# Attention: the products with the values of two steps issued together, every other step

## The chip, the cores and the metric

The kernel runs on one core of a Trainium2 chip. The metric is the device time in microseconds (us) of one execution. TensorE (PE in the profile; its weight loads are PEld), VectorE (DVE), ScalarE (ACT), GpSimd (POOL) and the queue of SyncE (SP) each work through their own list of instructions in order, and wait for one another through semaphores.

## The reference

Three stages follow each other: an attention within clusters, a gated feed-forward layer, and a mixture of eight experts. The change is in the first:

```python
mask = q_assign[:, :, :, None] == k_assign[:, :, None, :]      # clusters by the nearest centroid
scores = scale * np.matmul(q, k.transpose(0, 1, 3, 2))          # batch 2, 8 heads, 768 tokens, 64 wide
scores = np.where(mask, scores, -1000000000.0)
scores = scores - np.max(scores, axis=-1, keepdims=True)
attn = np.exp(scores)
attn = attn / (np.sum(attn, axis=-1, keepdims=True) + 1e-09)
return np.matmul(attn, v).astype(np.float32)
```

All of it is float32.

## The kernel before, in words

The attention works on pairs of heads: 2 batches times 4 pairs, eight in all. A pair's work is cut into 12 steps, two halves of 384 queries (`r`) times six blocks of 128 keys (`t`), so there are 96 steps. `plan` writes the order out by hand: `at(s, f, ...)` appends a piece of work to step `s`, and `advance` issues the steps one after the other, the pieces of a step in the order in which they were appended.

What a step issues, in order:

- `max_unit` (L332), 11 steps ahead of its use: two products `pm` (L344) of 128 queries with 768 keys, and on VectorE the row maximum `m` of them (L348).
- `score` (L369): four products `pst` (L379, L382), two for each head, and on ScalarE the exponential `P` (L386) out of PSUM into an SBUF tile. `P` has four buffers.
- `pv` (L400) of the step before: the products `acc` of the two heads' `P` with V (L410). Each head's output is 64 partitions of the one PSUM bank `acc`, which collects six steps (t = 0 to 5). A float32 product stands in the trace as two matmuls, so a call of `pv` is four `acc` matmuls. After t = 5 ScalarE copies the bank to `x` (L416).
- `add_up` (L389) of the step before: the running sum of the `P` tiles, on GpSimd, for three of the sixteen halves on VectorE.
- In some steps, `norm1` to `norm3`: the products `psum` with a matrix of ones (L423), of the same form as `acc`, and the reciprocal of the sums, which scales `x`.
- Behind these, the preparation of a later pair of heads, spread over 12 steps: transposes `pt` (L228) with the copy `qh` or `kh` on ScalarE and the subtraction `ql` or `kl` on VectorE, similarity products `psim` (L246), and others. `max_put` (L355) puts the negative maxima where the score products add them.

Two pieces of the feed-forward layer run beside it. `Narrow` turns the float64 weights into float32 with int32 operations `n` on ScalarE and VectorE (L663 to L690). From step 84 on, `Moe.first` issues the first products `ph` (L805) of the feed-forward layer between the steps; there are no more `max_unit` calls by then.

`pm` and `pst` tiles come from one function, which hands out two PSUM buffers of two banks each, in turn:

```python
    def big(self, name):
        self.nbig += 1
        return self.ps.tile([128, 2, 512], F32, tag=f"s{self.nbig % 2}", name=name)
```

The functions that the diff touches and what calls them:

Of the kernel before, what the change touches and what calls it, by code (L numbers as in the profile page):

```python
# [169 lines left out]
class Attention:  # L170
# [292 lines left out]
    def plan(self, N):  # L463

        NP = len(self.pairs)
        NS = 12 * NP
        steps = {}

        def at(s, f, *a):
            if s >= 0:  # L470
                steps.setdefault(s, []).append((f, a))

        for n in range(NS):
            at(n - self.AHEAD, self.max_unit, n)
        for s in range(NS):
            at(s, self.score, s)
        for s in range(NS):
            at(s + 1, self.pv, s)
            at(s + 1, self.add_up, s)
            if s % 6 == 5:  # L480
                for j, f in ((3, self.norm1), (4, self.norm2), (6, self.norm3)):
                    at(s + j, f, *divmod(s // 6, 2))
        for i in range(NP):
            end = 12 * i - self.AHEAD
            for r in range(2):
                at(end + 6 * r + 5, self.max_split, i, r)
                at(end + 6 * r + 6, self.max_put, i, r)
            base = end - 15 if i > 2 else self.B2
            if i > 1:
                at(base - 8, self.load, i, "qk")  # L490
                for j in range(4):
                    at(base + j, self.split, i, "qk"[j // 2], j % 2)
                for j in range(4):
                    at(base + 4 + j, self.sims, i, "qk"[j // 2], j % 2)
                at(base + 6, self.pick, i, "q")
                at(base + 8, self.pick, i, "k")
                at(base + 9, self.onehot_t, i)
                at(base + 10, self.first, i, 0)
                at(base + 11, self.first, i, 1)
                for h in range(2):  # L500
                    for kind in ("qa", "ka"):
                        at(base + 8, self.spread, i, (kind, h))
                    for kind in ("km", "qm"):
                        at(base + 12, self.spread, i, (kind, h))
            if i:
                for j, kind in enumerate(("ql", "qu", "kb", "kl")):
                    for h in range(2):
                        at(max(12 * i - 12, 3) + self.BS * j, self.spread, i, (kind, h))
            if i:
                at(12 * i - 12, self.load, i, "v")  # L510
        for c in range(3):
            at(self.N1, N.load, c)
        slots = [12 * p + w for p in range(NP) for w, m in enumerate(self.SLOTS) for _ in range(m)]
        slots = [w for w in slots if w >= self.N0]
        for c in range(N.CUT):
            s0, s1, s2 = slots[3 * c:][:3]
            for s, g in ((s0 - 1, N.bias), (s1 - 1, N.last), (s1, N.up), (s2, N.sign), (s2 + 1, N.store)):
                at(s, g, c)
            if c + 3 < N.CUT:
                at(s2 + self.NL, N.load, c + 3)  # L520
        return steps
# [1163 lines left out]
```

## Time and profile before

| | |
|---|---|
| time, median of 3 runs (lowest to highest) | 811.0 us (809.21 to 812.89) |
| time of the profiled execution | 809.26 us |
| its span, first to last instruction | 807.4 us |
| TensorE, VectorE, ScalarE, GpSimd busy | 95%, 76%, 58%, 27% of the span |
| mean granted clock of TensorE | 0.984 of full speed |

The attention steps take the stretch from 36.5 to about 298 us of the span. A busy share over the whole span is a mean over stages with different limits, so the attention stage is to be read by itself. Matmuls are pipelined: the duration of one in a row is longer than the distance to the next, and the distance of starts is what a row of matmuls costs. Where a row has "x4", four instructions of a line are merged, and the time is from the first start to the last end.

### The profile page before, as it was taken

To read this page: it belongs to the slowest core of one execution; us is meant where nothing else is said; L and a number is where in the kernel's file an instruction comes from. 1 tells how busy PE (TensorE), PEld (TensorE's weight loads), DVE (VectorE), ACT (ScalarE), POOL (GpSimd) and SP (SyncE) were. 2 spreads that over 40 slices of the span, in tenths; PEclk is the share of its full clock that TensorE was granted. 3 is DMA by queue.
4 is the path that set the end of the run, shared out by engine and by line. 5 is a ranking of instruction groups with operands and counts; after the bars stand their busy time and mean duration, and the time that the engine had idled before them with its cause. 6 is when DMAs were issued, how large, how long until landed. Compare 5 with 4: busy or idle time off the path is not lost.

```text
span 807.4 us, 12395 instructions
## 1 busy us (share of the span) xinstructions
PE 764.9 (95%) x4289; PEld 611.2 (76%) x4290; DVE 617.2 (76%) x1195; ACT 468.1 (58%) x899; POOL 218.4 (27%) x177
## 2 busy tenths in 40 slices
PE   7799899998999998989999999999999999999994
PEld 4465465655655566879889989999898999999993
DVE  5868889887898789999998588788667665566661
ACT  4167577675766675555656444455635566566551
POOL 5056577775777210011000002000131011101110
PEclk9999999999999999999999999999999999999997
DMA  7678878888675528778448058322427867887730
GB/s 162 163 193 240 204 201 230 194 228 206 187 201 147 186 98 311 288 268 333 157 167 290 11 195 270 138 105 64 134 92 227 280 209 225 271 264 220 215 122 22
DMA packets 118720, 155.77 MB, mean 193 GB/s; under 512 B 35033, under 2 KB 82233, under 8 KB 114555
## 3 DMA queue, kind: packets, MB, share of 16 engines
q1 hardware_dynamic: 113994, 131.83, 56.0%
q0 software_dynamic: 4656, 23.09, 7.2%
q8 instruction: 35, 0.57, 0.3%
q14 instruction: 35, 0.28, 0.1%
HBM read 93.65 MB, written 42.24 MB: 168 GB/s over the span
## 4 chain that ended last, share of the span: by engine, by line
PE 68%; DVE 18%; issue 5%; ACT 4%; DMA 3%; SPq 1%; POOL 0%; POOLq 0%; DVEq 0%; ACTq 0%
PE ph L805 12%; PE o L866 11%; PE he L1459 9%; PE y L1492 9%; PE acc L410 5%; PE pm L344 4%; PE pst L379 3%; DVE m L348 3%; PE pst L382 3%; PE psim L246 2%; DVE xl L459 2%; DVE cut L763 1%; DVE n L687 1%; DVE n L820 1%; DVE n L680 1%
## 5 line engine op out<-in xcount | busy, mean ns | idle before, releaser
L763 DVE TENSOR_TENSOR cut<-raw,cut 128x512 fp32r<-128x512 f32 x168 | 110.3, 687 | 27.9 <-ACT cut L762 15.4
L386 ACT ACTIVATE P<-pst 128x768 f32<-128x768 f32 x96 | 77.8, 810 | 63.9 <-PE pst L382 59.6
L398 POOL TENSOR_TENSOR sum<-sum,P 128x768 f32<-128x768 f32 x52 | 102.8, 1978 | 5.4 <-ACT P L386 2.6
L762 ACT ACTIVATE cut<-raw 128x512 fp32r<-128x512 f32 x168 | 98.3, 623 | 4.2 <-DMA raw<-in_moe_w_dram 4.2
L1492 PE MATMUL y<-cut,hy 128*128 128x512 f32 x384 | 99.3, 394 | 0.0
L348 DVE TENSOR_REDUCE m<-pm 128x1 f32<-128x768 f32 x96 | 90.7, 949 | 10.5 <-PE pm L344 10.2
L1459 PE MATMUL he<-xeh,cut 128*128 128x256 f32 x512 | 92.4, 280 | 0.2 <-ACT xeh L1413 0.2
L830 ACT ACTIVATE r<-n,two 128x384 f32<-128x384 f32 x64 | 39.5, 617 | 81.2 <-DVE n L820 80.1
L1459 PEld LDWEIGHTS he<-xeh,cut 128*128 128x128 f32 x512 | 82.2, 188 | 5.5 <-ACT xeh L1413 0.4
L410 PE MATMUL acc<-P,vn 128*64 128x384 f32 x384 | 83.7, 515 | 0.1
L1492 PEld LDWEIGHTS y<-cut,hy 128*128 128x128 f32 x384 | 67.6, 188 | 10.9
L805 PE MATMUL ph<-xh,cut 128*128 128x384 f32 x256 | 67.0, 343 | 6.0 <-DVE t L842 3.6
L1459 PE MATMUL he<-xel,cut 128*128 128x256 f32 x256 | 71.5, 279 | 0.2 <-DVE xel L1414 0.2
L344 PE MATMUL pm<-KA,QA 96*128 96x384 f32 x192 | 57.0, 379 | 14.4 <-DVE m L348 12.1
L379 PE MATMUL pst<-QB,KB 128*128 128x384 f32 x192 | 66.6, 347 | 1.1 <-issue 0.8
L805 PE MATMUL ph<-xh,again 128*128 128x384 f32 x256 | 66.7, 341 | 0.0
L1464 ACT ACTIVATE hy<-he 128x256 fp32r<-128x256 f32 x64 | 24.5, 383 | 70.5 <-PE he L1459 70.5
L382 PE MATMUL pst<-QA,KA 97*128 97x384 f32 x192 | 65.3, 340 | 0.0
L1504 POOL DMA_INDIRECT out_dram<-ye,meta x17 | 18.3, 1078 | 171.6 <-ACT ye L1502 154.0
L1465 DVE SCALAR_TENSOR_TENSOR hy<-he,hy 128x256 fp32r<-128x256 f32 x64 | 27.1, 424 | 43.9 <-ACT hy L1464 43.8
L866 PE MATMUL o<-cut,gh 128*128 128x512 f32 x192 | 59.8, 392 | 1.0 <-DVE rs L438 1.0
L866 PE MATMUL o<-again,gh 128*128 128x512 f32 x192 | 60.3, 395 | 0.0
(229 smaller groups left out, 1654.5 us busy)
## 6 DMA issues: line engine op xcount, KB each, us to landing
raw<-in_moe_w_dram SPq DMA_DIRECT2D x72, 256.0 KB
raw<-in_moe_w_dram SPq DMA_DIRECT2D x36, 512.0 KB
kept<-cut POOLq DMA_DIRECT2D x16, 1024.0 KB, 8.2
again<-kept SPq DMA_DIRECT2D x16, 1024.0 KB
n<-in_moe_w_in_dram SPq DMA_DIRECT2D x16, 512.0 KB
n<-in_moe_w_out_dram SPq DMA_DIRECT2D x16, 512.0 KB
wf<-n SPq DMA_DIRECT2D x32, 256.0 KB
raw<-wf SPq DMA_DIRECT2D x16, 512.0 KB
```

The lines of the kernel that those rows point to most:

```text
L344: nc.tensor.matmul(ps[:, g, 0:384], lhsT=QA[0:96, h, q0:q0 + 128], rhs=KA[0:96, h, 384 * g:384 * g + 384], start=True, stop=True,)
L348: nc.vector.reduce_max(out=st["m", r][:, h, t:t + 1], in_=ps[:, :, 0:384], axis=AX.XY)
L379: nc.tensor.matmul(ps[:, h, 0:384], lhsT=KB[:, h, ks], rhs=QB[:, h, qs], start=True, stop=False)
L382: nc.tensor.matmul(ps[:, h, 0:384], lhsT=KA[0:97, h, ks], rhs=QA[0:97, h, qs], start=False, stop=True)
L398: e.tensor_add(out=st["sum", r], in0=st["P", w - 1] if t == 1 else st["sum", r], in1=st["P", w])
L410: nc.tensor.matmul(acc[64 * h:64 * h + 64, 0:384], lhsT=st["v"][:, h, t, :], rhs=pt[:, h, :], start=(t == 0), stop=(t == self.NK - 1),)
L762: nc.scalar.activation(out=t[:, 0, part], in_=raw[:, part], func=AF.Copy)
L763: self.low.tensor_sub(out=t[:, 1, part], in0=raw[:, part], in1=f32(t[:, 0, part]))
L805: nc.tensor.matmul(ps[:, 0:384], lhsT=w[:, k, :], rhs=x[:, k, sl], start=(k == 0 and j == 0), stop=(k == 3 and j == 2),)
L866: nc.tensor.matmul(self.acc[t], lhsT=g[:, c], rhs=w, start=(f == 0 and j == 0), stop=(f == self.NF - 1 and j == 2),)
L1459: nc.tensor.matmul(ps[:, 0:MAIN], lhsT=w[:, k, :], rhs=x[:, k, :], start=(k == 0 and j == 0), stop=(k == 3 and j == 2),)
L1492: nc.tensor.matmul(st["y"][s], lhsT=g[:, c], rhs=w, start=(f == 0 and j == 0), stop=(f == 7 and j == 2))
```

## The change

In `plan`, the products with V of two steps are issued in one step. Before, step s + 1 issues `pv` of step s. Afterwards the steps with an odd s + 1 issue none, and those with an even s + 1 issue `pv` of s - 1 and of s, one behind the other. `add_up` stays in its step and now comes ahead of `pv`.

```diff
         for s in range(NS):
-            at(s + 1, self.pv, s)
             at(s + 1, self.add_up, s)
+            if s % 2:
+                at(s + 1, self.pv, s - 1)
+                at(s + 1, self.pv, s)
             if s % 6 == 5:
                 for j, f in ((3, self.norm1), (4, self.norm2), (6, self.norm3)):
                     at(s + j, f, *divmod(s // 6, 2))
```

## Rows read from the trace of the kernel before

**Rows 1.** The page: busy us of each engine, share of the span, instructions.
```profile
PE 764.9 (95%) x4289; PEld 611.2 (76%) x4290; DVE 617.2 (76%) x1195; ACT 468.1 (58%) x899; POOL 218.4 (27%) x177
```

**Rows 2.** Waits, 60 to 298 us: waiting <- releaser: us in total, times, longest.
```profile
PEld pm L344 <- DVE m L348: 25.3, 32, 2.9
```

**Rows 3.** Timeline of TensorE, step 58: start us, us, engine line op, out<-in.
```profile
203.52 0.34 PE L379 MATMUL pst<-QB,KB 128*128 128x384 f32 x1
...
204.05 0.34 PE L382 MATMUL pst<-QA,KA 97*128 97x384 f32 x1
204.31 0.87 PE L410 MATMUL acc<-P,vn 128*64 128x384 f32 x4
205.11 0.55 PE L228 MATMUL pt<-ident,qn 128*128 128x128 f32 x3
205.41 0.60 PE L344 MATMUL pm<-KA,QA 96*128 96x384 f32 x2
205.84 0.34 PE L379 MATMUL pst<-QB,KB 128*128 128x384 f32 x1
```

**Rows 4.** Timeline of TensorE, step 62, where psum and acc follow each other.
```profile
214.33 0.87 PE L423 MATMUL psum<-sum,ones 128*64 128x384 f32 x4
215.03 0.81 PE L410 MATMUL acc<-P,vn 128*64 128x384 f32 x4
215.77 0.38 PE L246 MATMUL psim<-cc,qh 128*128 128x256 f32 x1
...
216.58 0.51 PE L344 MATMUL pm<-KA,QA 96*128 96x384 f32 x2
```

**Rows 5.** Timeline of all engines, steps 57 to 59; in brackets, idle time and releaser.
```profile
202.73 0.68 DVE L680 SCALAR_TENSOR_TENSOR n<-n,n 128x512 int32<-128x512 int32 x1
...
204.48 0.81 ACT L386 ACTIVATE P<-pst 128x768 f32<-128x768 f32 x1 [1.01 <-PE pst L382]
204.58 8.06 POOL L398 TENSOR_TENSOR sum<-sum,P 128x768 f32<-128x768 f32 x4
...
204.72 2.23 DVE L687 SCALAR_TENSOR_TENSOR n<-n,n 128x512 int32<-128x512 int32 x1
...
205.69 0.49 ACT L234 ACTIVATE qh<-pt 128x384 fp32r<-128x384 f32 x1 [0.40 <-PE pt L228]
...
206.87 0.55 DVE L235 TENSOR_TENSOR ql<-pt,qh 128x384 fp32r<-128x384 f32 x1
...
207.34 0.94 DVE L348 TENSOR_REDUCE m<-pm 128x1 f32<-128x768 f32 x1
...
208.33 0.62 PE L344 MATMUL pm<-KA,QA 96*128 96x384 f32 x2 [0.34 <-DVE m L348]
```

**Rows 6.** Windows, steps 48 to 59, two steps each: stretch, length, busy us of each engine.
```profile
172.30:177.02 4.72, 4.72 (x29) 3.02 (x29) 3.95 (x7) 3.51 (x7) 4.64 (x3) 1.00 0.52 138
177.02:183.17 6.15, 6.15 (x37) 4.09 (x37) 4.30 (x7) 5.12 (x11) 2.66 (x3) 1.00 0.85 235
183.17:189.72 6.55, 5.80 (x33) 3.88 (x33) 6.38 (x8) 3.76 (x8) 6.39 (x4) 1.00 0.98 238
189.72:198.22 8.50, 6.30 (x29) 3.38 (x28) 6.06 (x9) 3.40 (x6) 4.08 (x3) 0.80 0.79 189
198.22:203.52 5.30, 5.30 (x28) 2.89 (x28) 4.23 (x7) 4.56 (x8) 1.01 (x1) 1.00 0.78 228
203.52:208.79 5.27, 4.93 (x27) 2.99 (x27) 5.27 (x6) 3.29 (x6) 5.02 (x4) 1.00 0.30 53
```
The columns of busy time are PE, PEld, DVE, ACT, POOL; then the granted clock, the DMA share and GB/s.

**Rows 7.** Windows, three of the six pairs in steps 72 to 83, same columns.
```profile
240.54:245.54 5.00, 4.43 (x23) 2.49 (x23) 4.84 (x6) 3.11 (x7) 4.84 (x3) 1.00 0.75 215
...
250.30:254.42 4.12, 4.12 (x22) 2.41 (x22) 2.73 (x4) 3.40 (x6) 3.58 (x3) 1.00 1.03 285
254.42:259.93 5.51, 4.44 (x23) 2.49 (x23) 4.85 (x5) 3.09 (x7) 5.35 (x3) 1.00 0.23 67
```

## Prediction, on record before the changed kernel ran

> **What bounds the kernel now.** I read the page first: TensorE is busy for 95% of the span and VectorE for 76% [rows 1], so a saving on TensorE can count, if nothing else ends last. Then the waits of the attention stage, where the change is: the largest wait of TensorE there is for VectorE's row maximum, 25.3 us in 32 cases [rows 2]. So TensorE sets the pace of most steps, and VectorE that of about a third. Third came TensorE's own timeline in one step [rows 3]. I let a step begin with the first pst product. Step 58 begins at 203.52, and the reader is to see five pieces without a gap: 0.53 us to the last pst product, 0.26 until acc starts, 0.80 until the transposes pt start, 0.30 until pm starts, 0.43 until the next step's first pst product; together 2.32 us.
>
> What hides behind that matters more. Every pm and every pst tile comes from the same two PSUM buffers in turn; a step takes one of each, so pm always gets the one and pst the other, and each is single-buffered. The next pst product can't start before the exponential P of this step is through, and the next pm not before this step's maximum m. P started at 204.48 and took 0.81, so it ended 1.77 us into the step [rows 5]; the next pst started at 2.32. Nobody waits for P today because the products with V and the transposes stand in between. That cover is what the change moves.
>
> **The change, part by part.** Removed, added: no instruction. 48 acc groups move from even to odd places, so each odd step loses its group and each even step has two. No DMA is issued by the moved function; the ScalarE copy of a finished acc stays in its step and comes later in it, and the next group's first product comes a step later than now, so it has more room. The adds change places with the products in the program only: they are on GpSimd or VectorE, whose order stays. P tiles of even steps live one step longer; four buffers hold that, since the products two steps on free them.
>
> *What a group costs.* A lone group costs 0.80, and 0.26 from the last pst product where the pst products follow each other at 0.53/3 = 0.18, so 0.08 for the change of shape: 0.88 leave an odd step [rows 3]. The cost of a second group right behind one is in the trace, since psum has the same form as acc: psum starts at 214.33, acc at 215.03, the next work at 215.77; two groups take 1.44, the second adds 0.64 [rows 4]. (By the start distance it would be 0.70; this is the other bound.) Were TensorE alone the limit, a pair of steps would win 0.88 - 0.64 = 0.24 us, and 48 pairs 11.5 us.
> The Trainium skill says in "TensorEngine Tiling (Array Packing)", Key Properties, that going from one tiling mode to another drains the engine. The trace agrees with its direction: the second group is 0.16 us cheaper than the lone one. By that rule alone the change would bring those 11.5 us; that is the first rival below.
>
> *What an odd step can win.* Without its group it needs 0.53 + 0.18 + 0.43 = 1.14 us and whatever else it holds. But pst of the next step waits for P: 1.77 plus the lag from a release to TensorE. The lag is not seen for P; for m it is 0.05 (m ends at 208.28, pm starts at 208.33) [rows 5], which I take, between 0 and 0.10. So an odd step takes at least 1.82 us. Other work in it of 0.68 us or more fills that; less does not.
>
> *Twelve steps of the steady part*, taken as pairs of an even and an odd step [rows 6]; their extra work repeats every twelve steps.
> - First pair (4.72 us, transposes in both). The odd step's maximum is queued on VectorE behind the subtraction of the transposes made in the even step. From the start of pt: 0.58 to the copy qh, 0.49 for it, 0.05 lag, 0.47 from the subtraction's start to that of m, 0.94 for m, 0.05 lag [rows 5], 0.43 from pm to the next pst product [rows 3]: 3.01 us. Now pt starts 0.53 + 0.26 + 0.80 = 1.59 into the step, and the chain ends at 4.60, inside the pair's 4.72. With two groups pt starts at 0.53 + 0.26 + 1.44 = 2.23 and the chain ends at 5.24: a loss of 0.52.
> - Second pair (6.15): both steps hold six psim products, together 0.81 us a step (215.77 to 216.58) [rows 4], over 0.68, so the odd step gets the full gain: -0.24.
> - Third and fourth pair (6.55 and 8.50): TensorE has idle time in them (5.80 and 6.30 busy), VectorE's queue sets the end. Its int32 operations n are the reason: one takes 0.68 alone (202.73) and 2.23 beside GpSimd's adds of P, which run at 2 us each (204.72) [rows 5]. I take 0. Bounds: both gains of 0.24 and one such hold-up of 2.23 - 0.68 = 1.55 avoided half the time, so about -1.2; or psim's 0.64 later start handed on to VectorE and half a hold-up more, about +1.4.
>   The Trainium skill explains the hold-up in "SBUF — State Buffer", Who interferes with whom: a VectorE instruction with two SBUF inputs and a GpSimd one that reads SBUF exclude each other for a whole instruction. The 2.23 beside 0.68 agrees; it means that small shifts come out in lumps here.
> - Fifth pair (5.30): the odd step has one small product besides, about as long as pt's 0.30. It goes from 2.32 to the floor of 1.82, -0.50; the even one +0.64: +0.14.
> - Sixth pair (5.27, transposes in both): the chain of the first pair, again 5.24: -0.03.
> Sum 0.52 - 0.24 + 0 + 0.14 - 0.03 = +0.39; six such twelves (steps 0 to 71): +2.3 us.
>
> *Steps 72 to 83* have no transposes and no psim [rows 7]. A plain step is 0.53 + 0.26 + 0.80 + 0.43 = 2.02 now (the pair 250.30 to 254.42 has 4.12 and no idle time). Odd: 2.02 to 1.82, -0.20; even: +0.64; +0.44 a pair. In two of the six pairs TensorE idles 0.57 and 1.07 us for VectorE, which swallows it: 0. Four pairs: +1.8 us.
>
> *Steps 84 to 95* have no pm, so pst alternates over both buffers, the floor is gone and each pair wins 0.24; the last two groups follow each other already, since no score comes after step 95. Five pairs: -1.2 us.
>
> *Sum:* 2.3 + 1.8 - 1.2 = +2.9 us. What follows the attention waits for it, since TensorE is busy through to the end, so it goes into the time. The profiled execution took 809.26 us, so one like it would take 812.2. It lies 1.7 below the median of the runs, 811.0, from which I state the forecast: 813.9 us.
>
> **The rivals.**
> *All of it is TensorE's.* The floor and the chain don't bind, and 48 x 0.24 = 11.5 us come off: 799.5. For it: TensorE has no gap in three of the six pairs [rows 6]. Against it: in an odd step of 1.14 us TensorE would have to write to the pst buffer some 0.6 us before ScalarE is through with it. 0.07. It is also what the rule on tiling modes in the Trainium skill ("TensorEngine Tiling (Array Packing)", Key Properties) would give.
> *The hold-ups fall better.* GpSimd's adds start later against VectorE's queue in the third and fourth pair, since the steps before end otherwise; six twelves at -1.2: 813.9 - 7.2 = 806.7. Nothing in the trace tells the direction. 0.10.
> *VectorE's queue becomes the bound* (the other side). In the third and fourth pair VectorE is busy 6.38 of 6.55 and 6.06 of 8.50 [rows 6]; if the psim products, 0.64 later in the even step, arrive when VectorE has nothing else, each twelve loses up to 1.4 there, and 1.0 in the mean gives 813.9 + 6.0 = 819.9. It decides from +0.2 us per twelve on, since +2.9 is near the limit of what counts as slower. With long waits comes the clock: in 189.72 to 198.22, after the two longest waits, the granted clock is 0.80 on average [rows 6]; that is the 1.2 GHz level for 40% of 8.50 us, at most 1.7 us of lost work each time. 0.30.
> *The forecast*, 811 to 818: 0.53.
>
> **How the numbers follow.** A measurement here tells 0.5%, 4 us, from no change. The forecast's case has some three quarters of its chance below 815.1 (+0.5%): 0.40 within, 0.13 slower. The third rival is slower, apart from 0.03; the first is faster; the second is faster in half. Faster 0.12, same 0.48, slower 0.40. The likeliest case's own range is 811 to 818. For 8 in 10 I go to 804, which takes in most of the second rival, and to 822, which takes in the third with one more fall of the clock. The second group at 0.70 instead of 0.64 adds up to 2.9 us, the lag of 0 to 0.10 some 1 us either way; both are inside.
>
> **What the new profile would show.** acc in groups of eight at a spacing of 0.64 to 0.70 us; acc gone from odd steps. Odd steps of about 1.82 us with a wait of pst for P that isn't there now, in steps with little else; odd steps that end on m where transposes came before. Even steps of 2.7 to 4.0 us. Wrong would be: odd steps well under 1.8 us before step 84 (then the floor is wrong and the first rival holds), or a total wait of TensorE for m that grows by more than 5 us, or falls (then the queue of VectorE and GpSimd decides).

## The result, and the profile after

The changed kernel takes 825.36 us (820.05 to 825.85, 3 runs), the kernel before 811.0; the ratio is 1.0141 (95% interval 1.0095 to 1.0186). The whole interval lies above 1: the kernel became slower, by some 1.4%, and the time is above the range of 804 to 822. The profiled execution is the one of 825.36 us.

The page's line on TensorE, to be held against [rows 1]:

```profile
PE 767.7 (93%) x4290; PEld 622.4 (76%) x4290; DVE 616.1 (75%) x1195; ACT 462.5 (56%) x899; POOL 218.9 (27%) x177
```

The same work, a longer span: all engines idle more. The first place to look is a plain odd step and the even one behind it, on TensorE and ScalarE (timeline of the changed kernel, steps 57 and 58; start, us, engine, line, and in brackets the idle time and its releaser):

```profile
211.50 0.34 PE L379 MATMUL pst<-QB,KB 128*128 128x384 f32 x1
...
212.46 0.81 ACT L386 ACTIVATE P<-pst 128x768 f32<-128x768 f32 x1 [1.08 <-PE pst L382]
...
213.32 0.19 PEld L379 LDWEIGHTS pst<-QB,KB 128*128 128x128 f32 x1 [0.32 <-ACT P L386]
213.32 0.44 PE L379 MATMUL pst<-QB,KB 128*128 128x384 f32 x1
213.60 0.34 PE L382 MATMUL pst<-QA,KA 97*128 97x384 f32 x1
...
214.23 1.51 PE L410 MATMUL acc<-P,vn 128*64 128x384 f32 x8
215.67 0.55 PE L228 MATMUL pt<-ident,qn 128*128 128x128 f32 x3
```

Step 57 has no acc. P ends at 213.27, pst starts at 213.32: the step takes 1.82 us, and the bracket names P. In step 58 two groups take 215.67 - 214.23 = 1.44. Both numbers are those of the forecast. One thing is new in this place: the weight load of a pst product that waits starts together with the product (both at 213.32), and the second one starts 0.28 behind the first instead of 0.18.

Then the twelve steps of [rows 6], steps 48 to 59, two by two (columns as there):

```profile
182.96:188.25 5.29, 4.75 (x28) 3.21 (x28) 4.50 (x7) 3.87 (x9) 5.07 (x4) 1.00 0.47 134
188.25:194.15 5.90, 5.90 (x37) 4.12 (x36) 4.31 (x7) 4.11 (x9) 2.41 (x2) 1.00 0.87 242
194.15:201.63 7.48, 5.55 (x34) 4.13 (x33) 6.74 (x8) 4.11 (x9) 6.64 (x4) 1.00 0.89 220
201.63:207.77 6.14, 4.60 (x28) 2.77 (x28) 6.06 (x9) 2.71 (x5) 2.27 (x2) 1.00 0.66 164
207.77:213.32 5.55, 5.48 (x27) 2.93 (x26) 4.39 (x6) 4.44 (x9) 2.84 (x2) 1.00 1.02 248
213.32:218.71 5.39, 4.75 (x28) 3.26 (x27) 3.95 (x7) 3.15 (x6) 4.72 (x3) 1.00 0.46 122
```

First, second, fifth and sixth pair came out at 5.29, 5.90, 5.55 and 5.39 where 5.24, 5.91, 5.44 and 5.24 were worked out. The third doesn't fit: 7.48 against 6.55, where I had taken 0. TensorE is busy for 5.55 of it. The fourth can't be compared exactly: the clock fell there in the kernel before [rows 6] and not now. But that fall cost at most the 1.7 us of the prediction, so at full clock the pair took 6.8 us or more before and takes 6.14 now: it became shorter.

Whole twelves, so that the clock can be kept out. First the kernel before (steps 24 to 35, 36 to 47, 60 to 71, 72 to 83, and the ten steps 84 to 93):

```profile
106.55:138.98 32.43, 31.59 (x176) 19.80 (x176) 28.04 (x41) 23.19 (x42) 22.85 (x14) 1.00 0.86 228
138.98:172.30 33.32, 31.84 (x176) 19.74 (x176) 30.13 (x42) 24.10 (x43) 24.68 (x16) 1.00 0.89 221
208.79:240.54 31.75, 31.00 (x169) 19.19 (x169) 27.11 (x39) 22.55 (x41) 22.41 (x14) 1.00 0.77 207
240.54:268.91 28.37, 26.66 (x131) 15.18 (x131) 25.94 (x30) 19.15 (x32) 19.94 (x12) 1.00 0.58 173
268.91:291.41 22.50, 22.47 (x114) 13.20 (x113) 16.33 (x26) 16.31 (x28) 4.58 (x5) 1.00 0.51 188
```

The changed kernel, the first two and the last of these stretches:

```profile
114.22:148.61 34.39, 30.89 (x175) 20.43 (x175) 27.96 (x41) 23.07 (x43) 23.97 (x16) 1.00 0.85 222
148.61:182.96 34.35, 30.79 (x175) 20.41 (x175) 28.37 (x42) 22.94 (x43) 23.89 (x14) 1.00 0.85 206
286.57:308.18 21.61, 21.26 (x114) 14.06 (x114) 16.26 (x26) 15.66 (x27) 4.33 (x5) 1.00 0.52 195
```

All of these rows are at full clock. The twelves lose 1.96 and 1.03 us, where +0.39 was forecast; the last stretch wins 0.89, where 1.2 was. The waits of TensorE for the row maximum, of the changed kernel from 60 to 315 us, answer to [rows 2] and show where the rest of the loss ends. In the first line, the kernel before once more, the wait as the products themselves see it; then the changed kernel:

```profile
PE pm L344 <- DVE m L348: 10.9, 11, 2.2
```

```profile
PEld pm L344 <- DVE m L348: 36.1, 35, 2.5
PE pm L344 <- DVE m L348: 23.5, 26, 1.9
PEld pst L379 <- ACT P L386: 4.7, 18, 0.3
```

The wait for P, which wasn't there, is 4.7 us in 18 cases; the wait for m grew from 25.3 to 36.1 us for the weight loads and from 10.9 to 23.5 us for the products. A growth of more than 5 us was the forecast's own sign that the queue of VectorE and GpSimd decides. So the main loss stands at VectorE's maximum, not at the floor.

**What the clock does to a time here.** The span ahead of step 0, where both programs are the same, was 36.52 us before and 39.10 after, and 39.50 in a later run of the changed kernel (e12). The granted clock goes with it: 0.95, 0.83 and 0.80. It isn't the change that does this: e9, an experiment on the kernel before, whose program is the same up to there, took 39.37 us at 0.75, and e5, with the change, 37.36 us at 0.87. One window each, before and e9; the clock is the third number from the end:

```profile
0.00:36.52 36.52, 27.20 (x138) 17.29 (x139) 24.48 (x61) 11.41 (x27) 11.20 (x19) 0.95 0.73 155
```

```profile
0.00:39.37 39.37, 32.50 (x138) 21.68 (x140) 24.76 (x60) 11.28 (x27) 11.18 (x19) 0.75 0.70 151
```

The mean clock of a run is in every result. The 73 runs of the kernel before that ran beside the experiments go from 807.87 us at 0.988 to 824.4 at 0.957; the straight line through them passes 814.8 us at 0.975 and rises by 5.3 us for each 0.01 that the clock falls, with a scatter of 1.2 us; without the two runs of them that count as slow it moves by less than 0.3 us. Below, "at equal clock" is the mean distance of a kernel's runs from that line. The three runs of the changed kernel lie 8.0 us above it. Their mean clock is 0.973; that of the three runs of before isn't recorded but for the profiled one, 0.984, and their median, 811.0, is where the line stands at 0.982. So of the 14.4 us, some 8 are there at equal clock and some 6 come with the clock.

### The profile page after: what moved, and what is told of

Same layout as the page of the kernel before. It is cut to its first block, busy times and chain, and to the rows that moved or that the text cites. A ratio compares the mean times of both kernels' runs of the same rounds, so it can differ in the third digit from the quotient of the medians.

```text
span 823.6 us, 12396 instructions
## 1 busy us (share of the span) xinstructions
PE 767.7 (93%) x4290; PEld 622.4 (76%) x4290; DVE 616.1 (75%) x1195; ACT 462.5 (56%) x899; POOL 218.9 (27%) x177
## 4 chain that ended last, share of the span: by engine, by line
PE 62%; DVE 19%; issue 8%; ACT 6%; DMA 2%; SPq 1%; POOL 1%; POOLq 0%; ACTq 0%; DVEq 0%
PE ph L807 11%; PE o L868 11%; PE he L1461 8%; PE y L1494 8%; PE acc L410 5%; DVE m L348 4%; PE pm L344 3%; PE pst L379 2%; PE pst L382 2%; PE psim L246 2%; DVE cut L765 2%; DVE n L822 1%; PE psum L423 1%; ACT r L832 1%; DVE xl L459 1%
## 5 line engine op out<-in xcount | busy, mean ns | idle before, releaser
L765 DVE TENSOR_TENSOR cut<-raw,cut 128x512 fp32r<-128x512 f32 x168 | 110.3, 687 | 27.6 <-ACT cut L764 14.4
L386 ACT ACTIVATE P<-pst 128x768 f32<-128x768 f32 x96 | 77.6, 809 | 73.8 <-PE pst L382 67.3
L344 PE MATMUL pm<-KA,QA 96*128 96x384 f32 x192 | 59.4, 393 | 26.7 <-DVE m L348 25.4
L410 PE MATMUL acc<-P,vn 128*64 128x384 f32 x384 | 74.7, 511 | 0.1
L379 PE MATMUL pst<-QB,KB 128*128 128x384 f32 x192 | 70.4, 367 | 1.8 <-issue 1.5
L382 PE MATMUL pst<-QA,KA 97*128 97x384 f32 x192 | 67.3, 350 | 0.0
L344 PEld LDWEIGHTS pm<-KA,QA 96*128 96x128 f32 x192 | 30.8, 200 | 45.8 <-DVE m L348 39.1
```

The source lines that it names most:

```text
L344: nc.tensor.matmul(ps[:, g, 0:384], lhsT=QA[0:96, h, q0:q0 + 128], rhs=KA[0:96, h, 384 * g:384 * g + 384], start=True, stop=True,)
L379: nc.tensor.matmul(ps[:, h, 0:384], lhsT=KB[:, h, ks], rhs=QB[:, h, qs], start=True, stop=False)
L382: nc.tensor.matmul(ps[:, h, 0:384], lhsT=KA[0:97, h, ks], rhs=QA[0:97, h, qs], start=False, stop=True)
L410: nc.tensor.matmul(acc[64 * h:64 * h + 64, 0:384], lhsT=st["v"][:, h, t, :], rhs=pt[:, h, :], start=(t == 0), stop=(t == self.NK - 1),)
L765: self.low.tensor_sub(out=t[:, 1, part], in0=raw[:, part], in1=f32(t[:, 0, part]))
```

## The experiments

| run | kernel | median us | ratio to before, 95% interval | at equal clock, us |
|---|---|---|---|---|
| e1 | changed, idle products in the waits | 831.74 | 1.0242 (1.0183 to 1.0301) | +20.1 |
| e2 | before, without most of GpSimd's adds | 798.8 | 0.9829 (0.9755 to 0.9903) | -14.8 |
| e3 | changed, without the same adds | 803.14 | 0.9869 (0.9807 to 0.993) | -8.6 |
| e4 | groups together in steps 71 to 84 only | 823.23 | 1.0136 (1.0078 to 1.0194) | +5.2 |
| e5 | changed, acc last in its step | 822.97 | 1.0145 (1.0095 to 1.0195) | +7.7 |
| e6 | before, acc last in its step | 815.25 | 1.0025 (0.9986 to 1.0064) | +1.9 |
| e7 | groups together from step 85 on only | 812.4 | 0.9984 (0.9948 to 1.0021) | -1.9 |
| e8 | changed, norm2 first in its step | 826.52 | 1.0179 (1.0136 to 1.0222) | +9.5 |
| e9 | before, norm2 first in its step | 812.68 | 0.9996 (0.9966 to 1.0027) | -2.2 |
| e10 | e7 and e9 together | 812.21 | 0.9962 (0.9927 to 0.9996) | -2.6 |
| e11 | e10, and together around step 3 of each twelve | 816.38 | 1.0015 (0.9984 to 1.0047) | -0.6 |
| e12 | the changed kernel again | 823.96 | 1.0172 (1.0131 to 1.0213) | +7.7 |

Three theories were to be told apart: A, the floor of the odd steps and the chains behind moved products cost more than worked out; B, VectorE's queue is held up longer behind GpSimd's adds; C, the longer waits let the clock fall. Each column of the table has its own weakness: the ratio contains where the clock fell, the last column rests on the line. Steps at full clock, read from the trace, need neither; where they decide, they are shown.

**e1: idle products in the waits of the changed kernel.** Is it the falling clock?

```diff
+    FILL = {1: 2, 5: 6, 6: 6, 9: 2, 11: 2}
...
+        for s in range(NS):
+            n = self.FILL.get(s % 12, 0) if s < 72 else (6 if s == 78 else 3 * (s % 2)) if s < 84 else 0
+            if n:
+                at(s, self.K.warm, n, None)
```

> The changed kernel with idle products (zeros, no use) put into TensorE's waits of the attention: two at the end of odd steps with little work, six at the end of the two steps in which it waits longest for the row maximum, three in odd steps from 73 on. They take 0.22 us each. Theory C (the fall of the clock in those waits costs 5 to 8 us of the 14): no stretch at 1.2 GHz between steps 13 and 84, the time 818 to 821 us. Theory B (the queue of VectorE and GpSimd costs it, the clock little): time 824 to 828, since the waits are as long as before.

Measured: 831.74 us, worse than either theory said. The clock's mean went up to 0.98, and still the kernel stands 20 us above the line. The idle products need a PSUM bank and got one that was still being read, as in step 57:

```profile
218.41 0.60 PE L50 MATMUL warm<-idle 128*128 128x512 bf16 x2 [0.54 <-DVE rs L438]
```

They waited for VectorE to read the bank, and pm, next in the queue, came late (218.66). The run doesn't price the clock, then, since the waits of the idle products can't be told from the change's own loss; it shows that a wait with in-order work behind it is no free room.

**e2 and e3: without GpSimd's adds.** Is it VectorE's hold-ups behind them?

```diff
-        if t == 0:
+        if t == 0 or t > 1 and s // 6 not in self.QUICK:
             return
```

> The kernel before, leaving out GpSimd's running sum of P from the third block of keys on (the sum is that of two blocks only). It takes away what holds VectorE's operations up. Theory B: TensorE's wait for the row maximum falls from some 36 us to under 12, the time to 800 to 804. Theory A (VectorE is simply full): little change, 808 to 812.

> The changed kernel, leaving out the same adds. To be read against e2. Theory B (the change costs by hold-ups of VectorE behind GpSimd, and by the clock that falls in the long waits after them): only the floor of the odd steps and the chain of the transposes stay, the difference to e2 is 0 to +4 us. Theory A (floor and chain cost more than I worked out): the difference stays at +9 us or more.

Without the adds the kernel before is 14.8 us faster at equal clock (798.8 us, a little below the 800 to 804), and TensorE waits for m for 6.1 us instead of 25.3: the hold-ups are real, and cost the kernel before as well. The third and fourth pair (steps 52 to 55) show what they do to the change. The third, first e2, then e3:

```profile
178.99:184.52 5.53, 5.53 (x34) 3.82 (x33) 4.62 (x9) 3.10 (x8) 0.76 (x1) 1.00 1.14 281
```

```profile
184.28:189.62 5.34, 5.34 (x34) 4.03 (x33) 3.98 (x8) 3.17 (x7) 1.01 (x1) 1.00 1.09 269
```

Without the adds the change wins 0.2 us in each of these pairs (the fourth goes from 4.76 to 4.57), as TensorE's own sum has it; with them it loses 0.93 in the third (6.55 to 7.48). There theory B holds. But the difference of the whole kernels at equal clock is still 6.2 us (4.3 between the medians), above the 0 to 4 that I had given it and below the 9 of theory A: without hold-ups TensorE is the limit of all other places too, so the floor and the chain cost where a wait for VectorE had hidden them before. Steps 72 to 83, e2 and e3, show it:

```profile
229.89:256.02 26.13, 26.07 (x131) 15.08 (x131) 21.93 (x30) 19.07 (x32) 6.14 (x5) 1.00 0.63 187
```

```profile
236.21:265.03 28.82, 26.98 (x132) 15.36 (x131) 22.21 (x30) 18.78 (x32) 5.87 (x5) 1.00 0.57 170
```

The six pairs lose 2.69 us, 0.45 each, where the forecast had worked out 0.44 for a plain pair. So the adds don't explain the loss by themselves; whichever wait is taken away, the odd step runs into the next.

**e4: the groups together in steps 71 to 84 only.**

```diff
-            if s % 2:
+            if not (lambda o: 71 <= o <= 83)(s | 1):
+                at(s + 1, self.pv, s)
+            elif s % 2:
                 at(s + 1, self.pv, s - 1)
                 at(s + 1, self.pv, s)
```

> The two groups issued together in steps 71 to 84 only, everything else in the order of before. Forecast's terms: +1.8 us in these steps, 812 to 813. Theory B with C: what the changed kernel shows there, +4.6 us in these steps, of which 1.5 is a fall of the clock after one long wait for VectorE: 814 to 816.

It took 823.23 us, more than either number; at equal clock it is +5.2. The rest goes with the clock, whose mean was 0.971; in the profiled run it stayed full in all the steps that differ from the kernel before. Its windows of steps 72 to 83, and of the pair 78 and 79 in them:

```profile
246.81:278.58 31.77, 26.66 (x131) 15.46 (x131) 27.61 (x30) 18.84 (x32) 19.78 (x12) 1.00 0.53 155
261.82:268.87 7.05, 4.29 (x22) 2.66 (x22) 6.51 (x6) 3.54 (x7) 4.90 (x3) 1.00 0.04 9
```

At full clock these steps lose 31.77 - 28.37 = 3.40 us, where +1.8 was forecast. The pair 78 and 79 has 1.54 of it: 7.05 against 5.51 [rows 7]. The changed kernel shows why:

```profile
267.12 6.14 POOL L398 TENSOR_TENSOR sum<-sum,P 128x768 f32<-128x768 f32 x3
...
267.51 1.97 DVE L682 SCALAR_TENSOR_TENSOR n<-n,n 128x512 int32<-128x512 int32 x1
...
269.41 2.17 DVE L459 SCALAR_TENSOR_TENSOR xl<-x,xh 128x384 fp32r<-128x384 f32 x1
271.50 0.94 DVE L348 TENSOR_REDUCE m<-pm 128x1 f32<-128x768 f32 x1
...
272.50 0.62 PE L344 MATMUL pm<-KA,QA 96*128 96x384 f32 x2 [1.88 <-DVE m L348]
```

VectorE's n takes 1.97 us and its xl 2.17 us beside the adds, m is queued behind them, pm waits for m. In the kernel before, the same n took 0.70 and xl 1.71; xl began 0.11 us into the pair there, and 1.21 here. The forecast had seen this wait and taken it for a cushion that would swallow the longer even step; it moved along with the step instead.

**e5 and e6: acc last in its step.** Does the loss come from the preparation products that now stand behind two groups?

```diff
-                at(s + 1, self.pv, s - 1)
-                at(s + 1, self.pv, s)
...
+        for s in range(1, NS, 2):
+            at(s + 1, self.pv, s - 1)
+            at(s + 1, self.pv, s)
         return steps
```

(In e6 the one group of every step is moved in the same way.)

> The changed kernel with the two groups moved to the end of their step, behind the transposes and similarity products, so that these are no longer 0.64 us later than before. Theory (chains: what is queued on VectorE behind those products sets the end of the next, odd step): the first pair of the twelve falls from 5.28 to about 4.8, the sixth from 5.38 to 4.8, and the third and fourth, whose subtractions come earlier too, lose part of the +0.9; the psum groups no longer stand beside acc, +0.24 twice. Sum about -1.5 per twelve, time 812 to 817 us. Rival (the floor of the odd steps and a full VectorE cost it, wherever the groups stand): all pairs within 0.1, 820 to 826.

> The kernel before with its one group moved to the end of every step in the same way, as the base for e5. Both theories: TensorE has the same work but for the psum groups that no longer stand beside acc (0.24 in two of twelve steps, +0.5 per twelve); VectorE gets its operands 0.8 us earlier and may win some of its waits back. 810 to 816 us.

Only the sixth pair of the twelve from step 48 did what I expected (5.39 to 4.91): there the chain of the transposes was the limit. The first didn't fall (5.29 to 5.42), and the third stands at 7.38, though its similarity products now come ahead of the groups. So their later start, which was how I had put the third rival, does not cost the third pair by itself. The sum, -1.5 per twelve, failed: +7.7 at equal clock, as the changed kernel. Against e6, its own base (+1.9, and within its 810 to 816 us), the groups together cost 5.8.

**e8 and e9: norm2 first in its step.** What does make GpSimd's adds fall worse?

```diff
+        for s in range(5, NS, 6):
+            late = steps[s + 4]
+            late.insert(0, late.pop(next(n for n, (f, a) in enumerate(late) if f == self.norm2)))
         return steps
```

> The changed kernel with the second part of the normalisation (which ends in GpSimd's two products with x, ahead of its adds) issued first in its step, ahead of the row maxima and the scores, so that it no longer waits on ScalarE behind the exponential of that step. Theory (the steps with psum are 0.64 us longer now, so the exponential, the products with x and the adds behind them come later on GpSimd, and VectorE's n is held up by the later add): GpSimd starts its adds some 1.3 us earlier, the third pair falls from 7.47 to 6.6 or less. Rival (VectorE has no room in that pair, wherever the adds lie): the third pair stays within 0.2 of 7.47. The time, 817 to 824 us, is no test.

> The kernel before with the normalisation moved in the same way, as the base for e8. Theory: the third pair, 6.55 in the kernel before, falls too, towards the 5.5 that it has without GpSimd's adds; the time 808 to 812 us. Rival: no change in that pair.

The same third pair, steps 64 and 65, in three kernels: GpSimd's product with x, VectorE's n and the maximum. Kernel before (the pair starts at 219.70):

```profile
219.45 1.01 POOL L447 TENSOR_TENSOR x<-x,rs 128x384 f32<-128x384 f32 x1 [1.97 <-ACT rs L446]
...
222.38 2.32 DVE L687 SCALAR_TENSOR_TENSOR n<-n,n 128x512 int32<-128x512 int32 x1
224.79 0.94 DVE L348 TENSOR_REDUCE m<-pm 128x1 f32<-128x768 f32 x1
```

Changed kernel (the pair starts at 229.88):

```profile
229.01 0.81 ACT L386 ACTIVATE P<-pst 128x768 f32<-128x768 f32 x1 [0.32 <-PE pst L382]
229.78 0.62 ACT L446 ACTIVATE rs<-rs,neg 128x384 f32<-128x384 f32 x1
...
230.54 1.00 POOL L447 TENSOR_TENSOR x<-x,rs 128x384 f32<-128x384 f32 x1 [2.61 <-ACT cl L252]
...
233.47 2.33 DVE L689 SCALAR_TENSOR_TENSOR n<-n,n 128x512 int32<-128x512 int32 x1
...
235.89 0.94 DVE L348 TENSOR_REDUCE m<-pm 128x1 f32<-128x768 f32 x1
```

Counted from the start of the pair, the product with x comes 0.25 us ahead of it in the kernel before and 0.66 behind it in the changed one, 0.91 later; n ends at 5.00 and at 5.92, 0.92 later; the maximum ends at 6.03 and at 6.95. That shift is the pair's loss. Of it, 0.64 is the second group in step 62; the other 0.3 is what steps 62 and 63 had just won (5.89 against 6.19 us), since the chain doesn't start from their end. One way by which it gets to GpSimd is ScalarE: rs (L446) is behind P (L386) in its queue, and P waits for a score that comes 0.64 later because the step ahead of it has two groups.

e8 puts rs ahead of P. Its third pairs, steps 52 and 64:

```profile
195.70:201.89 6.19, 5.54 (x33) 4.12 (x33) 6.04 (x8) 3.49 (x8) 6.03 (x4) 1.00 0.97 237
231.32:238.06 6.74, 5.56 (x34) 4.16 (x34) 6.65 (x9) 3.63 (x8) 6.58 (x4) 1.00 0.47 131
```

They fall from 7.48 to 6.19 and 6.74, on both sides of the 6.6 that I had given; the rival (VectorE has no room there) is out. But in e9 they fall too, as expected, from 6.55 to 5.70 and 6.22: the place of rs sets when the adds begin in both kernels, and the change still costs 0.5 in this pair. Second and third pair together (steps 50 to 53), without and with the groups together, first e9 and e8, then e6 and e5:

```profile
179.85:191.71 11.86, 11.86 (x70) 7.99 (x70) 9.84 (x15) 8.32 (x17) 9.03 (x6) 1.00 0.95 252
```

```profile
189.38:201.89 12.51, 11.68 (x69) 8.30 (x69) 10.35 (x15) 8.10 (x17) 9.04 (x6) 1.00 0.95 242
```

```profile
180.34:193.33 12.99, 12.09 (x70) 8.23 (x70) 10.76 (x15) 7.84 (x16) 8.89 (x6) 1.00 0.88 237
```

```profile
182.69:196.31 13.62, 11.78 (x69) 8.33 (x69) 11.23 (x15) 7.97 (x17) 9.27 (x6) 1.00 0.86 232
```

The change costs 0.65 and 0.63 us here, as in the kernels without either edit (12.70 to 13.38), and it wins 0.5 without the adds (e2 11.70, e3 11.18). So the adds carry the 0.64 us, and there are two ways to them: behind P on ScalarE, and behind the similarity products, whose qs (L253) stands ahead of rs (L438) in VectorE's queue. In the changed kernel both ways end together, P 0.05 us and VectorE's rs 0.13 us ahead of step 64. e8 closes the first way, e5 the second; no run closes both. In e8, besides, P waits behind rs on ScalarE (step 63 takes 2.25 us, 1.84 in the changed kernel), and the whole kernel is no better, +9.5 at equal clock. In the kernel before (e9) the edit brings 2.2 us at equal clock, which the ratio, 0.9996, doesn't show.

**e7, e10 and e11: where the change pays.** The selection is written as in e4, with `o >= 85` in e7, with e9's edit beside it in e10, and with `o >= 85 or o < 72 and o % 12 == 3` in e11.

> The two groups together only in the steps from 85 on, where no pm is left and pst has both buffers. Forecast's term: -1.2 us, 809.8 against 811.0; as the changed kernel shows these steps, -0.9. If the gain of 0.24 us for two groups side by side were wrong, 0.

> The kernel before with the normalisation first in its step (e9) and the two groups together from step 85 on (e7). Against the line of time over clock, e9 and e7 were 2.1 and 1.8 us faster each; they touch different steps, so the sum should be some 3.9 us, 0.5%, faster at equal clock. If what e9 gained is only a shift of hold-ups that comes back elsewhere, no more than 2 us.

> As e10, and the groups together also around the fourth step of each twelve (step 3 of 0 to 11), whose similarity products fill the floor: the one place of the steady part where the forecast and the changed kernel both have a gain (0.24 to 0.27 us a time, 1.5 in all). Theory (a group may leave a step only if other work of TensorE covers P and m there): 0 to 1.5 us faster than e10. Rival (the step that receives two groups is the one in front of VectorE's hold-ups, and its later similarity products cost more): 1 to 4 us slower than e10.

e7 is 1.9 us faster at equal clock; its ratio reaches over 1. Its trace shows the gain directly: from the start of step 84 to the end of the groups in step 94 it takes 23.08 us against 24.21 in the kernel before, 1.13 less at full clock, where the forecast had 1.2. e10 is the one kernel here that leaves nothing out and beats the kernel before beyond its interval, by 0.4%; against the line it has 2.6 us, less than the 3.9 expected. e11 is 2.0 us slower than e10. The second and third pair of the twelve from step 48 show why there is no gain: the pair in which a step loses its group gives 0.53 us (6.18 to 5.65), the one in which a step gets it costs 0.58 (5.70 to 6.28). The 0.24 is lost even here: the rival was right. Most of the 2.0 us is in one twelve, steps 36 to 47, first e10, then e11:

```profile
142.15:174.20 32.05, 31.36 (x176) 19.74 (x176) 27.45 (x42) 23.67 (x43) 25.12 (x15) 1.00 0.89 218
```

```profile
146.07:179.87 33.80, 31.30 (x175) 19.86 (x175) 29.38 (x42) 23.50 (x43) 24.88 (x15) 1.00 0.84 212
```

There an n that takes 0.68 us in e10 takes 2.35 beside the adds in e11, and the pair 42 and 43 takes 7.15 instead of 5.61.

**e12: the changed kernel again.**

> The changed kernel once more, beside the kernel before. Theory (8 us are the change's; the rest of the 14 is where the granted clock happened to fall, mostly ahead of the first step, where both programs are the same): the mean clocks of the two kernels agree within 0.004, the medians differ by 7 to 10 us, a ratio of 1.009 to 1.012. Rival (the longer waits make the clock fall more often in the changed kernel): its mean clock is lower by 0.008 or more, and the medians differ by 12 us or more.

823.96 against 812.5 us, a ratio of 1.0172; its runs have a mean clock of 0.969, those of the kernel before beside them 0.980. At equal clock it is +7.7, close to the 8.0 of the first three runs. So 8 us is what the change costs at one clock. But the theory failed by both of its conditions: the clock was lower by 0.011, and the ratio is above 1.012. The rival's condition on the clock holds; the medians differ by 11.5 us, just under its 12. One fall stands only in kernels with the change: in e12, as in the first profile and in e5, the 1.2 GHz level comes in step 79 or 80, after the wait of 1.88 us in step 78, which the kernel before doesn't have (pair 80 and 81 of e12, the clock is the third number from the end):

```profile
272.62:279.37 6.75, 6.40 (x25) 3.34 (x25) 4.74 (x7) 2.98 (x6) 1.00 (x1) 0.75 0.46 149
```

This pair has 5.15 us in e4 at full clock, so the fall costs 1.6. e4 has the wait too, 1.89 us, and no fall behind it, so the wait alone doesn't bring it. Most of the rest of the lower clock is ahead of step 0, where e9 has it as well. Whether the change makes the clock fall more often within the steps stays open.

## Why the prediction was wrong

**The floor and the chain of the transposes** were right where they bind: 1.82 us for the odd step, to the hundredth; first pair 5.29 (5.24 forecast), sixth 5.39 (5.24), fifth 5.55 (5.44, the 0.10 of the late weight load on top), the plain tail pair of steps 76 and 77 4.55 (2.66 + 1.82 = 4.48). That the floor is the wait for P is read from the trace; no run gave the pst tiles another buffer.

**The gain on TensorE** was right in size: two groups 1.44, second pair 5.90 (5.91), steps 84 to 93 -0.89, and e7 alone -1.13 (1.2 forecast).

**The step that failed is "I take 0"** for the third and fourth pair, and its like in the tail, "which swallows it: 0". I treated a wait for VectorE as a fixed end that absorbs what happens on TensorE ahead of it. But VectorE's queue in those pairs is held by GpSimd's adds, these by the product with x, this by rs, and that by work which the two groups ahead of it had made 0.64 us later, the exponential on ScalarE and the similarity products alike. The end moved with them: +0.9 in the third pair in four of the six twelves, +1.14 in the fourth pair of steps 42 and 43, +1.54 in steps 78 and 79. The bound of +1.4 was the right size; the choice of 0 inside it left the third pair out of the sum. The third rival, 819.9 us, had the right engine and the right price, and named one of two ways (the similarity products): e5, which moved them, left the way behind P as it was.

**One twelve stood for all six**, and that was a second error. The sixth pair, 5.27 us in [rows 6], takes 4.67 in steps 34 and 35 of the kernel before, so that the same chain, 5.39, costs 0.72 there and not nothing; it is part of the 1.96.

**The sum.** The twelves that can be compared at full clock lost 1.96 and 1.03; a third, steps 60 to 71 in e12, lost 1.80 (33.55 against 31.75):

```profile
217.50:251.05 33.55, 30.41 (x169) 19.68 (x169) 27.35 (x39) 22.05 (x41) 23.47 (x15) 1.00 0.72 196
```

In the others the clock fell in one of the two kernels. Steps 48 to 59 lost some 0.7 to 1.0, if the fall in the kernel before is taken off (36.50 less 1.5, by steps 18 and 19 below, to 1.7, against 35.75); steps 14 to 23 lay between -1.3 and +0.4 (e4 30.31; e12 30.69, with a fall in it). With some 1.0 in the mean for six, an estimate from these five, 2.9 in the tail (32.90 in e12 less the fall of 1.6, against 28.37) and -0.9 in the end it comes to 8 us. The line at equal clock says 8 too, and the forecast said 2.9.

**The clock** was priced in the forecast only as one more fall after a long wait. That there is one is right (1.6 us in step 80). That the clock ahead of the attention differs from run to run by as much as 3 us of time, I hadn't reckoned with: the 811.0 us from which I stated the forecast is the median of three runs among the shorter ones, where the median of the 73 later runs is 813.75 us. Beside such runs e12's ratio still says 1.7%.

**The rivals.** That all is TensorE's (799.5) fell with the first odd step: pst waits for P. That the hold-ups fall better did happen, but in two fourth pairs only: steps 54 and 55, shown above, and steps 18 and 19. There e4, which has the order of before, takes 7.03 us at full clock, and e12 6.39 us even at 0.73:

```profile
95.49:102.52 7.03, 4.83 (x29) 2.86 (x29) 6.06 (x9) 3.23 (x6) 3.13 (x3) 1.00 0.75 187
```

```profile
94.22:100.61 6.39, 5.99 (x29) 3.22 (x28) 6.14 (x9) 2.73 (x6) 2.27 (x2) 0.73 0.71 183
```

It didn't outweigh the third pairs.

## What to carry to other kernels

Work that stands between a producer and the reuse of its single buffer is cover; when it is moved to save a switch, first ask what waits in the step that it leaves: here 0.24 us saved in a pair against 0.68 us uncovered. A wait for a busy engine is no cushion unless that engine's queue starts from something that doesn't move; follow what holds it, engine by engine, back to a release that stays where it is, before "hidden" is written. And compare steps at the same granted clock, or many runs against their clock: of the 14 us between two medians of three runs here, some 6 went with the clock and not with the instructions.

## What the runs showed of the hardware

- Where a pst product waited for P, its weight load waited with it, and the second product started 0.28 us behind the first instead of 0.18 (step 58, and all 19 such waits of the changed kernel). The same 0.28 stands in the kernel before where pst follows acc directly.
- An int32 operation of 0.68 us on VectorE took 2.32 and 2.33 beside GpSimd's adds in kernels that were shifted against each other by 0.9 us: in both it ended 0.55 us behind the end of the add that ran when it started, so it doesn't slow down by a share, it waits for that add. The Trainium skill's rule for this pair ("SBUF — State Buffer", Who interferes with whom), one excludes the other for a whole instruction, agrees with that.
- The granted clock ahead of step 0 was 0.95, 0.83, 0.80 and 0.75 for the same instructions, which took 36.52 to 39.50 us.
